# Row transposes moved from TensorE to DMA crossbar transposes, with the down weights loaded in pieces

## The chip, the cores and the metric

The kernel runs on one core of one Trainium2 chip. The metric is the device time of one execution in microseconds (us), as the median of several. All runs compared here are fast runs: a full granted clock (0.98 or more in every run, 1.0 in nearly all).

## The reference

Input `x` has 2048 rows of 640. It is normalised by row, and the result goes two ways: through a two-dimensional Fourier transform, a multiplication by a complex weight for each frequency, and the inverse transform (A); and through two matmuls 640 to 1536 whose results are multiplied, and one back (B).

```python
def _A_ref(x, w_r, w_i):
    X = rfft2(x.astype(float32))            # over rows and columns
    X = X * (w_r + 1j * w_i)
    return irfft2(X, s=(S, D)).astype(bfloat16)

def _B_ref(x, w_gate, w_up, w_down):
    g = einsum("bsd,df->bsf", x, w_gate)    # 2048x640 by 640x1536
    u = einsum("bsd,df->bsf", x, w_up)
    return einsum("bsf,fd->bsd", g * u, w_down)

xn = layernorm(x)
return x + _A_ref(xn, A_w_r, A_w_i) + _B_ref(xn, B_w_gate, B_w_up, B_w_down)
```

## The kernel before

The 2048 rows are 16 row blocks of 128 ("rows 4" below means row block 4). A planner in the kernel takes a list of tasks with estimated durations and priorities and lays them out on the engines when the kernel is built, so a small edit can move many instructions. Everything in SBUF is one allocation, which the profile calls `arena`; PSUM is `ps`. The stages that matter here:

1. Layer norm of each row block on VectorE and ScalarE. Each normalised block is also transposed, since the gate and up matmuls contract over the 640 columns: five transposes by TensorE into PSUM, then one copy into SBUF.

```python
def em_t0(c, b=b):                                   # L813
    for j in range(5):
        ins = c.e.transpose(psb[:, bk * 1024 + j * 128: bk * 1024 + (j + 1) * 128],
                            v_x[:, b, j * 128:(j + 1) * 128], v_sm[:, 0, :])
...
def em_e0(c, b=b, t0=t0):                            # copy helper, L704 on ScalarE
    return copy_on(c, v_xt[:, :, b * 128:(b + 1) * 128], src)
```

2. Gate and up matmuls (L923), 1080 of them, wherever TensorE has nothing more urgent; ScalarE copies the results out and VectorE multiplies them (L938). The first transform runs beside them: VectorE combines rows (L837 to L871) and TensorE multiplies by tables (L884).
3. A loop over 16 frequency tiles: D (L964), weights (VectorE), C (L985 to L988), inverse (L1040, L1041). The inverse needs tables that lie where the down weights will lie later.
4. The down matmuls, two groups of 12 for each row block (L1140). A closing matmul (L1148) adds the inverse transform's result into the same PSUM group. VectorE prepares that result, two row blocks at a time: a matmul I (L1067) into PSUM, a copy, and then the steps V1 to V5 (L1089 to L1122). At last VectorE adds `x` and writes the result out of PSUM (L1155).

```python
b_wd = alloc("WD", 12 * 640)
b_ti = alloc("TI", 16 * 256, at=lay["WD"][0])        # inverse tables share the place
...
dma("ld_wd", v_wd, wdv, 1536 * 1280, [(b_wd, None)], prio=18.0)
...
for ft in range(12):                                 # down group, L1140
    ins = c.e.matmul(ps[:, bk, 0:320], v_ht[:, ft, a * 128:(a + 1) * 128], v_wd[:, ft, sl3],
                     start=(ft == 0), stop=False)
...
return c.e.tensor_tensor(v_out[:, a % 2, sl3], ps[:, bk, 0:320], v_xr[:, xs, sl3], _OP.add)   # L1155
```

Of the kernel before, what the change touches and what calls it, by code (L numbers as in the profile page):

```python
# [498 lines left out]
_X_LOADS = ((0, 1), (1, 1), (2, 1), (3, 1), (4, 4), (8, 8))  # L499
_LN_GROUPS = ((0, 1), (1, 1), (2, 1), (3, 1), (4, 2), (6, 2), (8, 2), (10, 2), (12, 2), (14, 2))  # L500
_NGW = 12
_NW = 4
_GW_LOADS = ((0, 2), (2, 2), (4, 2), (6, 2), (8, 4))
_CHUNKS = ((0, 1), (1, 1), (2, 2), (4, 2), (6, 2), (8, 2), (10, 2), (12, 2), (14, 2))
# [40 lines left out]
def _build(nc, A_x, A_w_r, A_w_i, B_w_gate, B_w_up, B_w_down, out, opts=None):  # L545
# [3 lines left out]
    with es:  # L549
# [19 lines left out]
            return sch.buf(name, off, size)  # L569

        b_ht = alloc("HT", 12 * 2048)
        b_xt = alloc("XT", 5 * 2048)
        b_gw = alloc("GW", 2 * 5 * _NGW * 128)
        b_u = alloc("U", 5 * 2048)
        b_v = alloc("V", 16 * 640, at=lay["U"][0])
        b_z2 = alloc("Z2", 5 * 2048)
        b_x = alloc("X", 16 * 640, at=lay["Z2"][0])
        b_wd = alloc("WD", 12 * 640)
        b_ti = alloc("TI", 16 * 256, at=lay["WD"][0])
        b_g = alloc("G", 640)  # L580
        b_sm = alloc("SM", 384)
        b_gbf = alloc("GBF", 6 * 512)
# [134 lines left out]
        for fi in range(opts.get("nfill", 70)):  # L717
            def em_fill(c):
# [3 lines left out]
                                  stop=True)  # L722
            T("fill%d" % fi, "pe", 2 * _d_mm(128), em_fill, prio=90.0 + 0.001 * fi, bank="single", cls="fill",
              selffree=True, reads=[(b_dum, None)])
        nwarm = opts.get("nwarm", 14)

        def em_warm(c):
            bk = bank_of(c.t)
# [2 lines left out]
                ins = c.e.matmul(ps[:, bk + (i % 2), (i % 4) * 128:(i % 4 + 1) * 128], v_dum[:, 0:128],  # L731
                                 v_dum[:, 128:256], start=True, stop=True)
            return ins
        T("warm", "pe", opts.get("warm_ns", 5200.0), em_warm, reads=[(b_dum, None)], prio=-1.0,
          bank="pair", cls="warm", selffree=True)

        def em_wpad(c):
# [8 lines left out]
        for gi, (b0, nb) in enumerate(_LN_GROUPS):  # L746
# [34 lines left out]

            def em_ve(c, sl_=sl_):
                return c.e.tensor_scalar(v_ve[:, sl_], v_mv[:, sl_, 1], 1e-5, None, _OP.add)
            T("ve_%d" % gi, "dve", 80.0, em_ve, reads=[(b_mv, gk)], writes=[(b_ve, gk)], prio=pbase)

            def em_sd(c, sl_=sl_):
                return c.e.activation(v_sd[:, sl_], v_ve[:, sl_], _ACTF.Sqrt)
            T("sd_%d" % gi, "act", 120.0, em_sd, reads=[(b_ve, gk)], writes=[(b_sd, gk)], prio=pbase)

            def em_rs(c, sl_=sl_):  # L790
                return c.e.reciprocal(v_rs[:, sl_], v_sd[:, sl_])
# [2 lines left out]
            for b in range(b0, b0 + nb):  # L794
                pb = pbase + 0.01 * (b - b0)

                def em_sub(c, b=b):
                    return c.e.tensor_scalar(v_x[:, b, :], v_x[:, b, :], v_mv[:, b, 0:1], None, _OP.subtract)  # L798
                T("sub%d" % b, "dve", 290.0, em_sub, reads=[(b_mv, ("b", b, b + 1))],
                  writes=[(b_x, ("s", b, b + 1))], prio=pb - 0.005)  # L800

                def em_mul(c, b=b):
                    if c.e is nc.scalar:
                        return c.e.activation(v_x[:, b, :], v_x[:, b, :], _ACTF.Copy, scale=v_rs[:, b:b + 1])
                    return c.e.tensor_scalar(v_x[:, b, :], v_x[:, b, :], v_rs[:, b:b + 1], None, _OP.mult)
                muls[b] = T("mul%d" % b, ("dve", "act") if b >= 4 else "dve", {"dve": 290.0, "act": _d_act(640) + 93}, em_mul, reads=[(b_rs, ("b", b, b + 1))],
                  writes=[(b_x, ("s", b, b + 1))], prio=pb)

                def em_t0(c, b=b):
                    bk = bank_of(c.t)  # L810
                    ins = None
                    for j in range(5):
                        ins = c.e.transpose(psb[:, bk * 1024 + j * 128: bk * 1024 + (j + 1) * 128],  # L813
                                            v_x[:, b, j * 128:(j + 1) * 128], v_sm[:, 0, :])
                    return ins
                t0 = T("T0_%d" % b, "pe", 5 * _d_mm(128), em_t0, reads=[(b_x, ("s", b, b + 1)), (b_sm, None)],
                       prio=pb, bank="single", cls="a")

                def em_e0(c, b=b, t0=t0):
                    bk = bank_of(t0)  # L820
                    src = psb[:, bk * 1024: bk * 1024 + 640].rearrange("p (j s) -> p j s", j=5)
                    return copy_on(c, v_xt[:, :, b * 128:(b + 1) * 128], src)
                e0 = T("eT0_%d" % b, ("act", "dve"), {"dve": _d_dve_psum16(640), "act": _d_act(640)}, em_e0,
                       writes=[(b_xt, ("s", b * 128, (b + 1) * 128))], prio=pb - 0.001, frees=t0)
                hold(t0, e0)


# [80 lines left out]
        for ui, (at_, ci, ft0) in enumerate(units):  # L908
            b0, nb = _CHUNKS[ci]
            n = 128 * nb  # L910
            rows = slice(b0 * 128, b0 * 128 + n)
            rr = ui % 3
            pu = 40.0 + 0.005 * ui
            pe_ = 5.0 + 0.001 * ui
            for u in range(2):
                ft = ft0 + u

                def em_gu(c, ft=ft, n=n, rows=rows):
                    bk = bank_of(c.t)
                    ins = None  # L920
                    for w in range(2):
                        for j in range(5):
                            ins = c.e.matmul(ps[:, bk, w * n:(w + 1) * n], v_gw[:, w, j, ft, :],  # L923
                                             v_xt[:, j, rows], start=(j == 0), stop=(j == 4))
                    return ins
                gu = T("GU_%d_%d" % (ft, b0), "pe", 10 * _d_mm(n), em_gu,
                       reads=[(b_gw, ("s", w_ * _NGW + ft, w_ * _NGW + ft + 1)) for w_ in range(2)] + [
                           (b_xt, ("s", b0 * 128, b0 * 128 + n))],
                       prio=pu + 0.001 * u, bank="single", cls="glu")

                def em_eg(c, gu=gu, rr=rr, n=n, u=u):
                    return copy_on(c, v_gbf[:, rr, u, 0:2 * n], ps[:, bank_of(gu), 0:2 * n])
                eg = T("eG_%d_%d" % (ui, u), ("act", "dve"), {"dve": _d_dve_psum(2 * n), "act": _d_act(2 * n)}, em_eg,
                       writes=[(b_gbf, ("r", 2 * rr + u, 2 * rr + u + 1))], prio=pe_, frees=gu)
                hold(gu, eg)

            def em_h(c, ft0=ft0, rr=rr, n=n, rows=rows):
                return c.e.tensor_tensor(v_ht[:, ft0:ft0 + 2, rows], v_gbf[:, rr, :, 0:n], v_gbf[:, rr, :, n:2 * n],  # L938
                                         _OP.mult)
            T("H_%d" % ui, "dve", _d_dve_tt16(2 * n), em_h,  # L940
              reads=[(b_gbf, ("r", 2 * rr, 2 * rr + 2))],
              writes=[(b_ht, ("col", b0, b0 + nb))], prio=pe_)


        dma("ld_ti", v_ti, d_ti, 128 * 16 * 512, [(b_ti, None)], prio=9.0)

        for t in range(16):
            pq = 10.0 + 0.05 * t
# [82 lines left out]
            def em_ia(c, t=t, r2=r2):  # L1031
                bk = bank_of(c.t)
                ins = None
                for k in range(5):
# [5 lines left out]
                    c.e.matmul(dst, l1, v_ti[:, t, 0, :], start=True, stop=False)  # L1040
                    ins = c.e.matmul(dst, l2, v_ti[:, t, 1, :], start=False, stop=True)  # L1041
                return ins
            ia = T("IA_%d" % t, "pe", 10 * _d_mm(128), em_ia, reads=[(b_y, ("r", 2 * r2, 2 * r2 + 2)), (b_ti, None)],
                   prio=pq, bank="pair", cls="a")

            def em_eia(c, ia=ia, t=t):
# [5 lines left out]
            hold(ia, eia)  # L1052


        dma("ld_wd", v_wd, wdv, 1536 * 1280, [(b_wd, None)], prio=18.0)
        for a in range(16):
            pa = 19.0 + 0.05 * a
            pc = 41.0 + 0.05 * a
# [68 lines left out]
        for a in range(16):  # L1127
# [4 lines left out]
            for hf in range(2):  # L1132
# [3 lines left out]
                def em_ag2(c, a=a, sl3=sl3):  # L1136
                    bk = bank_of(c.t)
                    ins = None
                    for ft in range(12):
                        ins = c.e.matmul(ps[:, bk, 0:320], v_ht[:, ft, a * 128:(a + 1) * 128], v_wd[:, ft, sl3],  # L1140
                                         start=(ft == 0), stop=False)
                    return ins
                ag2 = T("ACC_%d_%d" % (a, hf), "pe", 12 * _d_mm(320), em_ag2,
                        reads=[(b_ht, ("col", a, a + 1)), (b_wd, None)],
# [100 lines left out]
```

## Time and profile before

| | before |
|---|---|
| timed | 214.1 us median of 3 (214.05 to 214.6) |
| span of the profiled run | 212.6 us |
| TensorE | 2116 matmuls, busy 207.1 us (97%) |
| VectorE, ScalarE | busy 185.8 us (87%), 128.5 us (60%) |
| last first-transform matmuls start | 83.57 us |
| last inverse matmul done | 139.92 us |
| first down matmul | 149.23 us |

The prediction shows the lines of the engine table, the chain of waits and TensorE's timeline.

### The profile page before, as it was taken

To read this page: it belongs to the slowest core of one execution; us is meant where nothing else is said; L and a number is where in the kernel's file an instruction comes from. 1 tells how busy PE (TensorE), PEld (TensorE's weight loads), DVE (VectorE), ACT (ScalarE), POOL (GpSimd) and SP (SyncE) were. 2 spreads that over 40 slices of the span, in tenths; PEclk is the share of its full clock that TensorE was granted. 3 is DMA by queue.
4 is the path that set the end of the run, shared out by engine and by line. 5 is a ranking of instruction groups with operands and counts; after the bars stand their busy time and mean duration, and the time that the engine had idled before them with its cause. 6 is when DMAs were issued, how large, how long until landed. Compare 5 with 4: busy or idle time off the path is not lost.

```text
span 212.6 us, 5325 instructions
## 1 busy us (share of the span) xinstructions
PE 207.1 (97%) x2116; PEld 174.9 (82%) x2116; DVE 185.8 (87%) x535; ACT 128.5 (60%) x292; POOL 0.2 (0%) x4
## 2 busy tenths in 40 slices
PE   8999999999999999999999999999999999999994
PEld 8999899987878989889898888999767767777773
DVE  3599999999999997499999999839999999999621
ACT  2476899999998776779899888787212220200000
POOL 0000000000000000000000000000000000000000
DMA  6999991000000000012222220039112322333211
GB/s 191 303 341 392 393 294 33 0 0 3 0 5 0 3 0 0 3 38 59 56 58 53 57 55 9 3 100 375 39 46 80 108 79 63 108 96 101 84 48 46
DMA packets 22184, 19.78 MB, mean 93 GB/s; under 512 B 2192, under 2 KB 21264, under 8 KB 21904
## 3 DMA queue, kind: packets, MB, share of 16 engines
q1 hardware_dynamic: 20048, 18.37, 29.2%
q10 hardware_dynamic: 2112, 1.08, 1.9%
q8 instruction: 16, 0.26, 0.5%
q14 instruction: 8, 0.07, 0.1%
HBM read 16.82 MB, written 2.62 MB: 91 GB/s over the span
## 4 chain that ended last, share of the span: by engine, by line
PE 79%; DVE 17%; ACT 1%; issue 1%; DVEq 0%
PE ps L923 38%; PE ps L1140 21%; PE ps L731 3%; PE ps L1041 2%; PE ps L1040 2%; PE ps L1067 2%; PE ps L964 2%; DVE arena L938 2%; PE ps L1148 2%; PE ps L884 1%; DVE arena L837 1%; PE ps L813 1%; DVE arena L798 1%; PE ps L985 1%; PE ps L988 1%; PE ps L987 1%
## 5 line engine op out<-in xcount | busy, mean ns | idle before, releaser
L704 ACT ACTIVATE arena<-ps 128x512 bf16<-128x512 f32 (+5 forms) x200 | 107.1, 584 | 50.0 <-PE ps L1067 26.1
L923 PE MATMUL ps<-arena 128*128 128x256 bf16 (+1 forms) x1080 | 113.5, 261 | 0.8 <-ACT arena L704 0.8
L923 PEld LDWEIGHTS ps<-arena 128*128 128x128 bf16 x1080 | 93.6, 98 | 11.3 <-ACT arena L704 1.9
L1140 PE MATMUL ps<-arena 128*128 128x320 bf16 x384 | 56.7, 299 | 0.0
L1140 PEld LDWEIGHTS ps<-arena 128*128 128x128 bf16 x384 | 37.3, 98 | 14.2
L938 DVE TENSOR_TENSOR arena<-arena 128x512 bf16<-128x512 bf16 (+1 forms) x54 | 20.9, 390 | 10.0 <-ACT arena L704 9.7
L1000 DVE TENSOR_TENSOR arena<-ps,arena 128x256 f32<-128x256 f32 x64 | 22.6, 418 | 0.0
L1155 DVE TENSOR_TENSOR arena<-ps,arena 128x320 bf16<-128x320 f32 x32 | 15.5, 485 | 8.1 <-PE ps L1148 8.1
L1041 PE MATMUL ps<-arena 128*128 128x128 bf16 x80 | 10.6, 219 | 0.0
L1040 PE MATMUL ps<-arena 128*128 128x128 bf16 x80 | 10.6, 219 | 0.0
L1148 PE MATMUL ps<-arena 128*128 128x320 bf16 x32 | 9.6, 299 | 0.0
L1040 PEld LDWEIGHTS ps<-arena 128*128 128x128 bf16 x80 | 8.8, 112 | 0.4
L837 DVE TENSOR_TENSOR arena<-arena 128x384 f32<-128x384 bf16 x16 | 8.9, 554 | 0.0
L1041 PEld LDWEIGHTS ps<-arena 128*128 128x128 bf16 x80 | 8.7, 113 | 0.1
L731 PE MATMUL ps<-arena 128*128 128x128 bf16 x56 | 6.1, 313 | 1.0 <-DVE arena L738 1.0
L1003 DVE TENSOR_TENSOR arena<-ps,arena 128x260 f32<-128x260 f32 x16 | 7.1, 444 | 0.0
L1015 DVE TENSOR_TENSOR arena<-arena 128x256 bf16<-128x256 f32 x16 | 6.8, 423 | 0.2
L1024 ACT ACTIVATE arena<-arena 128x256 bf16<-128x256 bf16 x16 | 6.6, 415 | 0.3 <-DVE arena L1019 0.2
L757 ACT ACTIVATE arena<-arena 128x640 bf16<-128x640 bf16 x8 | 6.8, 845 | 0.0
L731 PEld LDWEIGHTS ps<-arena 128*128 128x128 bf16 x56 | 5.9, 150 | 1.0 <-DVE arena L738 1.0
L838 DVE TENSOR_TENSOR arena<-arena 128x256 f32<-128x256 bf16 x16 | 6.7, 421 | 0.0
L1019 DVE TENSOR_TENSOR arena<-arena 128x256 bf16<-128x256 f32 x16 | 6.7, 420 | 0.0
(71 smaller groups left out, 224.2 us busy)
## 6 DMA issues: line engine op xcount, KB each, us to landing
arena<-in_A_x_dram SPq DMA_DIRECT2D x20, 160.0 KB, 3.0
out_dram<-arena SPq DMA_DIRECT2D x32, 80.0 KB, 1.6
arena<-in_B_w_down_dram SPq DMA_DIRECT2D x1, 1920.0 KB, 9.1
arena<-c_tf SPq DMA_DIRECT2D x4, 384.0 KB, 11.2
arena<-in_A_w_r_dram SPq DMA_DIRECT2D x32, 40.1 KB, 2.2
arena<-in_A_w_i_dram SPq DMA_DIRECT2D x32, 40.1 KB, 2.2
arena<-in_B_w_gate_dram SPq DMA_DIRECT2D x4, 320.0 KB, 7.5
arena<-in_A_x_dram SPq DMA_DIRECT2D x1, 1280.0 KB, 12.1
```

The lines of the kernel that those rows point to most:

```text
L704: return c.e.activation(dst, src, _ACTF.Copy)
L731: ins = c.e.matmul(ps[:, bk + (i % 2), (i % 4) * 128:(i % 4 + 1) * 128], v_dum[:, 0:128], v_dum[:, 128:256], start=True, stop=True)
L837: c.e.tensor_tensor(uo[:, o, :, 0:3, :], v_xb[:, b:b + 2, 0:6:2, :], v_xb[:, b:b + 2, 5:10:2, :], op)
L923: ins = c.e.matmul(ps[:, bk, w * n:(w + 1) * n], v_gw[:, w, j, ft, :], v_xt[:, j, rows], start=(j == 0), stop=(j == 4))
L938: return c.e.tensor_tensor(v_ht[:, ft0:ft0 + 2, rows], v_gbf[:, rr, :, 0:n], v_gbf[:, rr, :, n:2 * n], _OP.mult)
L1000: c.e.tensor_tensor(v_p[:, r2, w, :, 128 * h:128 * h + 128].rearrange("p c (m k) -> p c m k", k=4), xh.rearrange("p c (m k) -> p c m k", k ...
L1003: ins = c.e.tensor_tensor(v_p[:, r2, :, :, 256:321], ps[:, bk:bk + 2, 256:321].unsqueeze(1).to_broadcast([128, 2, 2, 65]), v_w[:, wr, :, 0 ...
L1040: c.e.matmul(dst, l1, v_ti[:, t, 0, :], start=True, stop=False)
L1041: ins = c.e.matmul(dst, l2, v_ti[:, t, 1, :], start=False, stop=True)
L1140: ins = c.e.matmul(ps[:, bk, 0:320], v_ht[:, ft, a * 128:(a + 1) * 128], v_wd[:, ft, sl3], start=(ft == 0), stop=False)
L1148: return c.e.matmul(ps[:, bank_of(ag2), 0:320], v_sm[:, 2, :], v_v[:, a, sl3], start=False, stop=True)
L1155: return c.e.tensor_tensor(v_out[:, a % 2, sl3], ps[:, bk, 0:320], v_xr[:, xs, sl3], _OP.add)
```

## The change

Its intent: take 60 of the 80 row transposes and their copies off TensorE, ScalarE and VectorE, and let the DMA crossbar do them from SBUF to SBUF. With less TensorE work in front, fewer gate and up matmuls are left to cover the late load of the down weights, so that load is cut: 800 KB (tiles 7 to 11) go early into the part that the inverse tables leave free, the rest follows in four pieces as the tables are used up. Third, the transposes of rows 0 and 1 are copied out by ScalarE (two tiles) and VectorE (three) at once, into separate buffers, and the warm-up is 8 matmuls shorter.

```diff
+_WD_LOADS = ((7, 12), (0, 2), (2, 4), (4, 6), (6, 7))
+_FT_ORDER = (7, 8, 9, 10, 11, 0, 1, 2, 3, 4, 5, 6)
...
-        nwarm = opts.get("nwarm", 14)
+        nwarm = opts.get("nwarm", 12)
...
+                if b >= opts.get("xt_dma", 4):
+                    def em_xt(c, b=b):
+                        return c.e.dma_start_transpose(v_xt[:, :, b * 128:(b + 1) * 128], v_x[:, b, :])
+                    T("xt%d" % b, "sp", opts.get("xt_issue", 1500.0), em_xt, reads=[(b_x, ("s", b, b + 1))],
+                      writes=[...], prio=pb, nbytes=128 * 1280)
+                    continue
...
+                if b < opts.get("e0_split", 2):
+                    for part, (j0, j1) in (("act", (0, 2)), ("dve", (2, 5))):
+                        def em_e0s(c, b=b, t0=t0, j0=j0, j1=j1):
...
+                            return copy_on(c, v_xt[:, j0:j1, b * 128:(b + 1) * 128], src)
...
-        dma("ld_wd", v_wd, wdv, 1536 * 1280, [(b_wd, None)], prio=18.0)
+        for f0, f1 in _WD_LOADS:
+            dma("ld_wd%d" % f0, v_wd[:, f0:f1], wdv[:, f0:f1], 128 * (f1 - f0) * 1280,
+                [(b_wd, ("e", 640 * f0, 640 * f1))], prio=18.0 if f0 < 7 else 9.6)
...
-                    for ft in range(12):
+                    for ft in _FT_ORDER:
```

Left out: the load of the inverse tables in two halves, finer dependencies on the tables, and slightly earlier priorities for two tiny layer-norm steps. In the changed kernel the same code has other line numbers: row transposes L828, crossbar transposes L816, gate and up L951, first transform L912, inverse L1070 and L1071, I L1099, V1 to V5 L1121 to L1154, down L1172, closing L1180, result L1187.

More of the change, by code (lines that the diff above doesn't have):

```diff
@@ L571, in _build @@
         b_ht = alloc("HT", 12 * 2048)
-        b_xt = alloc("XT", 5 * 2048)
+        b_xta = alloc("XTA", 2 * 2048)
+        b_xtb = alloc("XTB", 3 * 2048)
+        lay["XT"] = (lay["XTA"][0], 5 * 2048)
         b_gw = alloc("GW", 2 * 5 * _NGW * 128)
@@ L578, in _build @@
         b_wd = alloc("WD", 12 * 640)
-        b_ti = alloc("TI", 16 * 256, at=lay["WD"][0])
+        b_ti = b_wd
+        lay["TI"] = (lay["WD"][0], 16 * 256)
         b_g = alloc("G", 640)
@@ L733, in em_warm @@
             return ins
-        T("warm", "pe", opts.get("warm_ns", 5200.0), em_warm, reads=[(b_dum, None)], prio=-1.0,
+        T("warm", "pe", opts.get("warm_ns", 5050.0), em_warm, reads=[(b_dum, None)], prio=-1.0,
           bank="pair", cls="warm", selffree=True)
@@ L783, in em_ve @@
                 return c.e.tensor_scalar(v_ve[:, sl_], v_mv[:, sl_, 1], 1e-5, None, _OP.add)
-            T("ve_%d" % gi, "dve", 80.0, em_ve, reads=[(b_mv, gk)], writes=[(b_ve, gk)], prio=pbase)
+            T("ve_%d" % gi, "dve", 80.0, em_ve, reads=[(b_mv, gk)], writes=[(b_ve, gk)], prio=pbase - 0.006)
             def em_sd(c, sl_=sl_):
                 return c.e.activation(v_sd[:, sl_], v_ve[:, sl_], _ACTF.Sqrt)
-            T("sd_%d" % gi, "act", 120.0, em_sd, reads=[(b_ve, gk)], writes=[(b_sd, gk)], prio=pbase)
+            T("sd_%d" % gi, "act", 120.0, em_sd, reads=[(b_ve, gk)], writes=[(b_sd, gk)], prio=pbase - 0.006)
             def em_rs(c, sl_=sl_):
@@ L807, in _build @@
                   writes=[(b_x, ("s", b, b + 1))], prio=pb)
+                if b >= opts.get("xt_dma", 4):
+                    def em_xt(c, b=b):
+                        return c.e.dma_start_transpose(v_xt[:, :, b * 128:(b + 1) * 128], v_x[:, b, :])
+                    T("xt%d" % b, "sp", opts.get("xt_issue", 1500.0), em_xt, reads=[(b_x, ("s", b, b + 1))],
+                      writes=[(b_xta, ("s", b * 128, (b + 1) * 128)), (b_xtb, ("s", b * 128, (b + 1) * 128))], prio=pb, nbytes=128 * 1280)
+                    continue
                 def em_t0(c, b=b):
@@ L812, in em_t0 @@
                     for j in range(5):
-                        ins = c.e.transpose(psb[:, bk * 1024 + j * 128: bk * 1024 + (j + 1) * 128],
+                        o_ = j * 128
+                        if b < opts.get("e0_split", 2):
+                            o_ = j * 128 if j < 2 else 1024 + (j - 2) * 128
+                        ins = c.e.transpose(psb[:, bk * 1024 + o_: bk * 1024 + o_ + 128],
                                             v_x[:, b, j * 128:(j + 1) * 128], v_sm[:, 0, :])
@@ L816, in _build @@
                 t0 = T("T0_%d" % b, "pe", 5 * _d_mm(128), em_t0, reads=[(b_x, ("s", b, b + 1)), (b_sm, None)],
-                       prio=pb, bank="single", cls="a")
+                       prio=pb, bank="pair" if b < opts.get("e0_split", 2) else "single", cls="a")
+                if b < opts.get("e0_split", 2):
+                    for part, (j0, j1) in (("act", (0, 2)), ("dve", (2, 5))):
+                        def em_e0s(c, b=b, t0=t0, j0=j0, j1=j1):
+                            bk = bank_of(t0)
+                            o_ = bk * 1024 + (1024 if j0 else 0)
+                            src = psb[:, o_: o_ + (j1 - j0) * 128].rearrange("p (j s) -> p j s", s=128)
+                            return copy_on(c, v_xt[:, j0:j1, b * 128:(b + 1) * 128], src)
+                        n_ = (j1 - j0) * 128
+                        es_ = T("eT0_%d_%s" % (b, part), part, {"dve": _d_dve_psum16(n_), "act": _d_act(n_)}, em_e0s,
+                                writes=[(b_xta if j0 == 0 else b_xtb, ("s", b * 128, (b + 1) * 128))], prio=pb - 0.001, frees=t0)
+                    hold(t0, es_)
+                    continue
                 def em_e0(c, b=b, t0=t0):
@@ L823, in _build @@
                 e0 = T("eT0_%d" % b, ("act", "dve"), {"dve": _d_dve_psum16(640), "act": _d_act(640)}, em_e0,
-                       writes=[(b_xt, ("s", b * 128, (b + 1) * 128))], prio=pb - 0.001, frees=t0)
+                       writes=[(b_xta, ("s", b * 128, (b + 1) * 128)), (b_xtb, ("s", b * 128, (b + 1) * 128))], prio=pb - 0.001, frees=t0)
                 hold(t0, e0)
@@ L927, in _build @@
                        reads=[(b_gw, ("s", w_ * _NGW + ft, w_ * _NGW + ft + 1)) for w_ in range(2)] + [
-                           (b_xt, ("s", b0 * 128, b0 * 128 + n))],
+                           (b_xta, ("s", b0 * 128, b0 * 128 + n)), (b_xtb, ("s", b0 * 128, b0 * 128 + n))],
                        prio=pu + 0.001 * u, bank="single", cls="glu")
@@ L942, in _build @@
               writes=[(b_ht, ("col", b0, b0 + nb))], prio=pe_)
-        dma("ld_ti", v_ti, d_ti, 128 * 16 * 512, [(b_ti, None)], prio=9.0)
+        for q in range(2):
+            dma("ld_ti%d" % q, v_ti[:, 8 * q:8 * q + 8], d_ti[:, 8 * q:8 * q + 8], 128 * 8 * 512,
+                [(b_wd, ("e", 2048 * q, 2048 * q + 2048))], prio=9.0 + 0.3 * q)
         for t in range(16):
@@ L1042, in em_ia @@
                 return ins
-            ia = T("IA_%d" % t, "pe", 10 * _d_mm(128), em_ia, reads=[(b_y, ("r", 2 * r2, 2 * r2 + 2)), (b_ti, None)],
+            ia = T("IA_%d" % t, "pe", 10 * _d_mm(128), em_ia, reads=[(b_y, ("r", 2 * r2, 2 * r2 + 2)), (b_wd, ("e", 256 * t, 256 * t + 256))],
                    prio=pq, bank="pair", cls="a")
@@ L1138, in em_ag2 @@
                     ins = None
-                    for ft in range(12):
+                    for ft in _FT_ORDER:
                         ins = c.e.matmul(ps[:, bk, 0:320], v_ht[:, ft, a * 128:(a + 1) * 128], v_wd[:, ft, sl3],
-                                         start=(ft == 0), stop=False)
+                                         start=(ft == 7), stop=False)
                     return ins
```

## The prediction

> **What bounds the kernel now.** I read the page's table of engines first, then its chain, then the waits of TensorE, then the timeline of TensorE with its gaps added up by hand.
>
> ```profile
> span 212.6 us, 5325 instructions
> ...
> PE 207.1 (97%) x2116; PEld 174.9 (82%) x2116; DVE 185.8 (87%) x535; ACT 128.5 (60%) x292; POOL 0.2 (0%) x4
> ...
> PE 79%; DVE 17%; ACT 1%; issue 1%; DVEq 0%
> ```
>
> TensorE is nearly always busy and carries 79% of the chain. Busy time of pipelined matmuls is not work, though, so I count start to start, from the timeline:
>
> ```profile
> 22.83 3.44 PE L923 MATMUL ps<-arena 128*128 128x256 bf16 x30
> 26.11 0.72 PE L813 MATMUL ps<-arena 128*128 128x128 bf16 x10
> 26.66 6.44 PE L923 MATMUL ps<-arena 128*128 128x256 bf16 x90
> 32.94 0.72 PE L884 MATMUL ps<-arena 128*128 128x128 bf16 x10
> ```
>
> Columns are start, length, engine, line, shape, count. Thirty gate/up matmuls 256 wide take 26.11 - 22.83 = 3.28 us, 109 ns each; ten 128 wide (row transposes, L813) 26.66 - 26.11 = 0.55, 56 ns each; in the same way 136 ns for 320 or 321 columns. With the counts of the program: gate/up 840 x 0.109 + 240 x 0.056 = 105.1; down 416 x 0.136 = 56.6; row transposes 80 x 0.056 = 4.5; the other transforms 400 x 0.056 + 64 x 0.1365 = 31.1; fillers 20 x 0.056 = 1.1. Sum 198.3 us. The warm-up (56 matmuls, start 1.05 to the first row transpose at 7.18) takes 6.1. The last matmul ends at 209.98, so 209.98 - 1.05 - 198.3 - 6.1, some 4.5 us, is all that TensorE loses over the whole run, and the rest after it is a 2.6 us tail. No large wait is left to remove: only work, and small stalls. Named waits are tiny:
>
> ```profile
> PE ps L731 <- DVE arena L738: 1.0, 1, 1.0
> PE ps L923 <- ACT arena L704: 0.8, 2, 0.6
> PE ps L1067 <- DVE arena L1099: 0.5, 1, 0.5
> ```
>
> Second bound: VectorE. From 33 to 62 us it is as full as TensorE, and ScalarE too:
>
> ```profile
> core 0: us, PE busy (x) PEld busy (x) DVE busy (x) ACT busy (x) POOL busy (x), PEclk, DMA share, GB/s
> ...
> 33.00:62.00 29.00, 28.73 (x297) 24.69 (x295) 28.76 (x94) 28.52 (x65) 0.00 (x0) 1.00 0.01 3
> 62.00:86.00 24.00, 24.00 (x246) 21.48 (x244) 21.33 (x56) 18.30 (x33) 0.00 (x0) 1.00 0.00 1
> ```
>
> VectorE's chain of layer norm and first transform (L837 to L871) ends about 83.0 us, and the last first-transform matmuls (L884) follow at 83.57: VectorE paces the start of the loop over frequency tiles, and TensorE stays full only because gate/up matmuls fill in.
>
> **What the Trainium skill says.** "VectorE: DVE Perf Modes", The three transpose paths, gives 1309 ns for a 128x128 bf16 transpose by the DMA crossbar and 390 ns by TensorE. In this trace TensorE's transposes are pipelined at 56 ns, so the measurement decides there; no run so far shows a crossbar transpose. "Advanced Engine Details and Errata", X-Bar Transpose (TRN2), says that transposes run as fast as ordinary DMAs, 350 to 400 GB/s. The two pages differ by more than ten for one row block of five tiles (6.5 us against 0.5 us), which is my largest uncertainty. "DMA: Bandwidth & Descriptors", Issuing engines are not separate DMA queues, says that all DMAs share the same 16 engines; the trace agrees in that the inverse tables, issued at 17.6 us, land 15.2 us later, behind everything before them. "TensorE: Matmul & The Clock Gate", Part 1, says the array runs at half rate until about 3.4 us of sustained work; here the warm-up runs at 109 ns per 128-wide matmul (half rate) up to about 6.9 us, so it takes longer than the page says.
>
> **The change, part by part.**
>
> Transposes removed: 12 rows x 5 = 60 matmuls x 56 ns = 3.36 us of TensorE, on the path. Their copies out of PSUM, some 12 x 0.6 us, were nearly all ScalarE's; that relieves an engine that is full from 33 to 62 us and may give back some 0.3 us of hidden stalls, no more. VectorE gains nothing: the built order of instructions gives it 3 copies of first transposes (two of three tiles, about 0.27 us each, one of five, 0.40) where it had two (0.80).
>
> Start: 8 warm-up matmuls fewer x 109 ns = 0.87 us. The first normalised row is ready at 5.98 us (L805 at 5.59, 0.39 long), so the first transpose can start at 6.3, though at half rate (0.55 us in place of 0.28). Its copy is split: ScalarE took 0.70 us (7.50 to 8.20). VectorE's part stands behind row 1's statistics, which end about 7.2 us, so it ends near 7.5, and gate/up starts near 7.6 instead of 8.41. Row 1's normalisation then waits 0.27 us for that copy, so part is given back in the layer-norm chain. I count 0.6 us.
>
> Down weights: before, one load of 1920 KB is issued at 140.1 us, after the last use of the inverse tables, and lands 9.1 us later. TensorE covers that with 70 gate/up matmuls, 7.6 us, so it costs nothing now. In the changed order only 30 gate/up matmuls stand after the last inverse matmul; the other 40 go before the frequency loop. So the piecewise load is what makes the removal usable rather than a gain itself. The last piece (160 KB; loads of that size land in 3.0 us) depends on the last inverse matmul; TensorE has 10 + 10 + 10 gate/up and 20 inverse matmuls (3.3 + 1.1 = 4.4 us) before the first down matmul: hidden.
>
> Loop over frequency tiles: 300 gate/up matmuls lie in it in both orders, with the same VectorE work: unchanged.
>
> Where the loop starts: TensorE work before the last first-transform matmuls is 510 x 0.109 instead of 470 x 0.109 (+4.4 us), minus 3.36, minus 0.6: it arrives where it did before, about 83.7. VectorE's work up to there, summed from the built order with the trace's durations, is 0.8 us more (two more gate/up products of 0.34 and the copy), 0.3 us earlier at best: about 83.5 to 84. So the loop starts within 0.5 us of where it did, near 84.1 at the end of those matmuls. From there the old kernel took 209.98 - 84.12 = 125.86 us; 40 gate/up matmuls fewer, 4.4 us: 121.5. End 205.6, plus the 2.6 tail: span 208.2. The timed median exceeded the profiled span by 1.5 us (214.1 - 212.6): **209.7 us**. The other way round: 4.5 - (3.36 + 0.6 = 4.0) leaves the same small losses as before.
>
> **The rivals.**
>
> A: the first crossbar transposes come late. They stand on the queue behind all loads, now with 800 KB of down weights among them. DMA traffic before drains at 32.5 us:
>
> ```profile
> 31.50:32.00 0.50, 0.50 (x13) 0.50 (x10) 0.48 (x2) 0.38 (x3) 0.00 (x0) 1.00 1.14 171
> 32.00:32.50 0.50, 0.50 (x12) 0.41 (x9) 0.50 (x3) 0.33 (x2) 0.00 (x0) 1.00 0.62 116
> 32.50:33.00 0.50, 0.50 (x12) 0.50 (x11) 0.40 (x2) 0.50 (x2) 0.00 (x0) 1.00 0.35 86
> ```
>
> The second last column is the DMA share, the last GB/s. 0.82 MB at 390 GB/s adds 2.1 us: about 34.7. Rows 4 and 5 then land near 37 if a transpose moves as a copy does. Gate/up of these rows starts after 29.6 us of TensorE work from the first transpose; with the first-transform matmuls of rows 2 and 3 held by VectorE to about 33.5, that is 36.8 to 37.4. So a stall of 0 to 1.5 us, in full on the path: 209.7 to 211.2. For it: the transposes are issued after their loads. Against: the later ones have 10 us and more to spare.
>
> B: crossbar transposes at 1.3 us per tile, one after another: row 4 lands about 41, row 5 near 48, a stall of some 11 us: about 221. The later rows need one pair per 14 us and would just keep up. I give it 1 in 20.
>
> C: VectorE becomes the bound: TensorE's saving returns as waits before the frequency loop and in the last transform (L1089 to L1122), where TensorE lost 0.7 us between 150 and 160 with more filler than it has now. If half the saving goes there: 211.7. Against: TensorE now has three down groups ahead of the first closing matmul, so 9.9 us after the last inverse matmul, and VectorE needed 10.0 with two more products in between.
>
> D: everything goes well, the stalls in 47 to 61 and at 160 us go too: 208.3.
>
> **Range and chances.** 209.7, with A and C to the upper side more than D to the lower: 208.2 to 213.0. Faster by 2% means under 209.8, right at my number: 0.46 faster, 0.49 the same, 0.05 slower (B).
>
> **What would show it right or wrong.** The row transposes should fall to 20, 60 matmuls fewer. TensorE's first gate/up near 7.6 us. At the first gate/up of rows 4 and 5 (about 37 us) there should be at most a wait of 1.5 us on a crossbar transpose; time from issue to landing of these should be 2 to 5 us. The last first-transform matmuls near 84 us. The first down matmul some 4.4 us after the last inverse one, without a wait on a load. A wait over 3 us on a crossbar transpose, or idle TensorE before L1187's partner matmuls (L1180), would make the number wrong.

## The result, and the profile after

The changed kernel takes 213.21 us (median of 4, 212.72 to 213.35), the kernel before in the same rounds 214.18 us (median of 4). The ratio is 0.9947, with a 95% interval of 0.9925 to 0.9969. Ratios and intervals here are worked out from all fast runs of the same rounds, so a ratio is not quite that of the medians quoted. The change wins about 1 us where 4.4 were predicted. It is "the same" at the 2% bar, and the time lies 0.2 us above the range of 208.2 to 213.0 that was given.

The page of the changed kernel, engine table and chain by engine:

```profile
span 211.5 us, 5204 instructions
...
PE 202.6 (96%) x2044; PEld 169.4 (80%) x2044; DVE 185.1 (87%) x536; ACT 122.1 (58%) x281; POOL 0.2 (0%) x4
...
PE 67%; DVE 22%; DMA 6%; issue 3%; ACT 1%; SPq 0%; DVEq 0%
```

TensorE has 72 matmuls fewer (60 transposes, 8 of warm-up, 4 fillers), so the work did go. But the chain carries 67% of TensorE in place of 79%, 22% of VectorE in place of 17%, and 6% of DMA, which was not in it before. Removed work came back as waits, and those have names. TensorE's waits (total, times, longest) in the changed kernel:

```profile
PE ps L951 <- DMA arena<-arena: 1.2, 1, 1.2
...
PE ps L951 <- DVE arena L775: 0.9, 1, 0.9
PE ps L1099 <- DVE arena L1131: 0.7, 2, 0.4
...
PE ps L1180 <- DVE arena L1154: 0.4, 1, 0.4
PE ps L1172 <- DVE arena L1187: 0.3, 1, 0.3
```

**The start.** TensorE and VectorE in the first ten microseconds, two answers of the timeline:

```profile
5.88 0.44 PE L828 MATMUL ps<-arena 128*128 128x128 bf16 x5 [0.55 <-DVE arena L810]
...
8.16 1.28 PE L951 MATMUL ps<-arena 128*128 128x128 bf16 x20 [0.95 <-DVE arena L775]
```

```profile
6.87 0.49 DVE L769 BATCH_NORM_STATS2 arena<-arena 128x6 f32<-128x320 bf16 x1 [1.14 <-DMA arena<-in_A_x_dram]
7.28 0.48 DVE L770 BATCH_NORM_STATS2 arena<-arena 128x6 f32<-128x320 bf16 x1
7.68 0.34 DVE L710 COPY arena<-ps 128x384 bf16<-128x384 bf16 x1
```

The first row's transposes start at 5.88 us, 1.1 us earlier than before (6.99). Gate and up start at 8.16 where before had 8.41: only 0.25 us is left. TensorE's wait is put down to L775, the short step that follows on VectorE, but what was missing is the copy L710 at 7.68. It stands behind row 1's two statistics in VectorE's order, and these waited 1.14 us for row 1's load. VectorE was free all that time, and the tiles that it had to copy were in PSUM from about 6.3 (5.88 + 0.44).

This is one execution of each kernel, and the start differs from one to the next. In the five other profiles with the same split (e1, e3, e4, e5 and e6 below), row 1's load lands earlier and gate and up start at 7.65 to 7.83; in e8, which has the start of the kernel before, they start at 7.64 and not at 8.41. By the first pair of first-transform matmuls, with the same gate/up matmuls and row transposes in front of it in both kernels, the difference is 0.32 us:

```profile
22.27 0.72 PE L884 MATMUL ps<-arena 128*128 128x128 bf16 x10
21.95 0.72 PE L912 MATMUL ps<-arena 128*128 128x128 bf16 x10
```

**The crossbar.** TensorE where rows 4 and 5 are due and at the last first-transform matmuls (these in the kernel before as well, L884), and the crossbar transposes by themselves (issue time on the queue in ns as minimum, median and maximum, then first and last start; below it issue to landing):

```profile
34.43 3.44 PE L951 MATMUL ps<-arena 128*128 128x256 bf16 x30
39.07 6.91 PE L951 MATMUL ps<-arena 128*128 128x256 bf16 x60 [1.21 <-DMA arena<-arena]
45.91 0.73 PE L912 MATMUL ps<-arena 128*128 128x128 bf16 x10
...
85.37 0.72 PE L912 MATMUL ps<-arena 128*128 128x128 bf16 x10
```

```profile
83.57 0.72 PE L884 MATMUL ps<-arena 128*128 128x128 bf16 x10
```

```profile
L816 SPq DMA_TRANSPOSE arena<-arena x12: 1200/1210/1721, 32.2 to 66.5; - x12
DMA to landing us min/median/max: 2.6/2.7/6.5
```

TensorE stands still for 1.21 us. The last first-transform matmuls, at 83.57 before, start at 85.37, so the loop starts 1.8 us later. The landing of 6.5 us is that of the first transpose (the second takes 5.1); the median is 2.7. The wait, too, differs between executions: e4 and e6, with the same order in this part, show 0.7 us of it and last first-transform matmuls at 84.71 and 84.89.

**The loop.** From the end of those matmuls to the last inverse matmul, before took 139.92 - 84.12 = 55.80 us and the changed kernel takes 141.71 - 85.93 = 55.78.

**The end.** The last inverse matmul to the start of the last closing matmul: 209.57 - 139.92 = 69.65 us before, 208.54 - 141.71 = 66.83 after. TensorE's work there, start to start: 415 down and closing matmuls x 0.1358 = 56.36, 80 of I x 0.056 = 4.48, and gate/up 70 x 0.109 = 7.63 before, 30 x 0.109 = 3.27 after. So the work is 68.5 and 64.1 us, and TensorE loses 1.2 us before and 2.7 after. The 1.2 us before are three gaps, all in front of the matmuls I (L1067, at 152.95, 159.51 and 173.28). Busy time of each engine (length of the stretch, PE, PEld, DVE, ACT, POOL, clock, DMA share, GB/s), first before:

```profile
150.00:170.00 20.00, 19.45 (x160) 14.07 (x159) 19.83 (x48) 3.93 (x7) 0.00 (x0) 1.00 0.23 67
170.00:190.00 20.00, 19.88 (x159) 14.45 (x157) 19.97 (x50) 2.60 (x4) 0.00 (x0) 1.00 0.30 87
```

and after:

```profile
150.00:170.00 20.00, 18.74 (x153) 13.17 (x152) 19.93 (x50) 3.90 (x6) 0.00 (x0) 1.00 0.25 74
170.00:190.00 20.00, 19.54 (x155) 14.00 (x154) 19.96 (x49) 2.60 (x4) 0.00 (x0) 1.00 0.27 79
```

VectorE is full in both kernels. What differs is whether TensorE has other work meanwhile. In the changed kernel the chain runs on VectorE from 153.8 to 189.2 us, and TensorE waits in small pieces, like this first one at the second pair of row blocks:

```profile
158.11 0.45 PE L1180 MATMUL ps<-arena 128*128 128x320 bf16 x2 [0.41 <-DVE arena L1154]
```

Before, TensorE reached its first down matmul at 149.23 and VectorE's first pair was ready at 149.88 (L1122 ends), only 0.65 us behind. After, TensorE comes at 146.10 and VectorE's first pair is ready at 151.04 (L1154 ends), 4.9 us behind:

```profile
149.23 1.80 PE L1140 MATMUL ps<-arena 128*128 128x320 bf16 x12
149.46 0.42 DVE L1122 TENSOR_TENSOR arena<-arena 128x256 bf16<-128x256 f32 x1
146.10 1.79 PE L1172 MATMUL ps<-arena 128*128 128x320 bf16 x12
150.62 0.42 DVE L1154 TENSOR_TENSOR arena<-arena 128x256 bf16<-128x256 f32 x1
```

The first two lines are of the kernel before, the others of the changed one. VectorE needs 6.74 us for a pair (L1123 at 158.65, then 165.39) and TensorE 52 x 0.1358 + 10 x 0.056 = 7.62, so VectorE makes up some 0.9 us in each pair, and the waits end only after several pairs.

So the theory was: 1.8 us are lost before the loop (crossbar wait and start) and 1.5 us at the end (VectorE's pace). The rivals: the crossbar itself is too slow, or the removed transposes cost nothing before, since VectorE paces everything.

### The profile page after: what moved, and what is told of

It is laid out like the page before. It is cut to its first block, busy times and chain, and to the rows that moved or that the text cites. A ratio compares the mean times of both kernels' runs of the same rounds, so it can differ in the third digit from the quotient of the medians.

```text
span 211.5 us, 5204 instructions
## 1 busy us (share of the span) xinstructions
PE 202.6 (96%) x2044; PEld 169.4 (80%) x2044; DVE 185.1 (87%) x536; ACT 122.1 (58%) x281; POOL 0.2 (0%) x4
## 4 chain that ended last, share of the span: by engine, by line
PE 67%; DVE 22%; DMA 6%; issue 3%; ACT 1%; SPq 0%; DVEq 0%
PE ps L951 41%; PE ps L1172 12%; DMA arena<-arena 3%; DMA arena<-in_A_x_dram 2%; PE ps L1070 2%; PE ps L1071 2%; DVE arena L1187 2%; PE ps L994 2%; PE ps L912 2%; DVE arena L1144 1%; DVE arena L1145 1%; DVE arena L1153 1%; DVE arena L1137 1%; PE ps L1015 1%; ACT arena L709 1%
## 5 line engine op out<-in xcount | busy, mean ns | idle before, releaser
L709 ACT ACTIVATE arena<-ps 128x512 bf16<-128x512 f32 (+5 forms) x189 | 99.9, 572 | 55.0 <-PE ps L1099 28.2
L951 PE MATMUL ps<-arena 128*128 128x256 bf16 (+1 forms) x1080 | 112.8, 261 | 2.8 <-DMA arena<-arena 1.2
L951 PEld LDWEIGHTS ps<-arena 128*128 128x128 bf16 x1080 | 93.6, 98 | 14.2 <-ACT arena L709 1.6
L1172 PE MATMUL ps<-arena 128*128 128x320 bf16 x384 | 56.5, 299 | 0.3 <-DVE arena L1187 0.3
L1172 PEld LDWEIGHTS ps<-arena 128*128 128x128 bf16 x384 | 37.2, 98 | 14.7 <-DVE arena L1187 0.7
L1187 DVE TENSOR_TENSOR arena<-ps,arena 128x320 bf16<-128x320 f32 x32 | 15.4, 482 | 6.7 <-PE ps L1180 6.7
L1071 PE MATMUL ps<-arena 128*128 128x128 bf16 x80 | 10.7, 219 | 0.0
L1070 PE MATMUL ps<-arena 128*128 128x128 bf16 x80 | 10.6, 219 | 0.0
L1180 PE MATMUL ps<-arena 128*128 128x320 bf16 x32 | 9.1, 300 | 0.5 <-DVE arena L1154 0.4
L1070 PEld LDWEIGHTS ps<-arena 128*128 128x128 bf16 x80 | 8.7, 112 | 0.5
L1071 PEld LDWEIGHTS ps<-arena 128*128 128x128 bf16 x80 | 8.7, 112 | 0.1
L769 DVE BATCH_NORM_STATS2 arena<-arena 128x6 f32<-128x320 bf16 x8 | 3.9, 489 | 3.8 <-DMA arena<-in_A_x_dram 3.7
L1152 DVE TENSOR_TENSOR arena<-arena 128x640 bf16<-128x640 f32 x8 | 6.5, 818 | 0.1
(71 smaller groups left out, 212.2 us busy)
## 6 DMA issues: line engine op xcount, KB each, us to landing
arena<-c_ti SPq DMA_DIRECT2D x2, 512.0 KB, 14.5
```

The source lines that it names most:

```text
L709: return c.e.activation(dst, src, _ACTF.Copy)
L951: ins = c.e.matmul(ps[:, bk, w * n:(w + 1) * n], v_gw[:, w, j, ft, :], v_xt[:, j, rows], start=(j == 0), stop=(j == 4))
L1070: c.e.matmul(dst, l1, v_ti[:, t, 0, :], start=True, stop=False)
L1071: ins = c.e.matmul(dst, l2, v_ti[:, t, 1, :], start=False, stop=True)
L1180: return c.e.matmul(ps[:, bank_of(ag2), 0:320], v_sm[:, 2, :], v_v[:, a, sl3], start=False, stop=True)
```

## The experiments

Eight kernels were run, in two sets of four. In the first the kernel before had a median of 214.32 us (11 runs), in the second 214.45 us (11 runs). All the edits but the last are to the changed kernel, which was not run again in these sets: a gain over it is a comparison across sets, by the ratios to the kernel before (its own is 0.9947, 0.9925 to 0.9969). Where the intervals overlap, as for e2 and e3, the times alone do not show a difference from it.

| run | median us (runs) | ratio to before | 95% interval |
|---|---|---|---|
| e1_late_down | 212.35 (6) | 0.9905 | 0.9885 to 0.9925 |
| e2_whole_copy | 212.56 (6) | 0.9917 | 0.9893 to 0.9940 |
| e3_no_xbar | 213.89 (6) | 0.9973 | 0.9953 to 0.9993 |
| e4_short_tail | 210.62 (5) | 0.9817 | 0.9793 to 0.9841 |
| e5_one_down | 214.52 (4) | 1.0032 | 0.9997 to 1.0068 |
| e6_act_out | 212.12 (5) | 0.9896 | 0.9879 to 0.9913 |
| e7_all_three | 211.05 (4) | 0.9841 | 0.9826 to 0.9856 |
| e8_before_act_out | 215.41 (6) | 1.0056 | 1.0037 to 1.0076 |

### e1_late_down: the early down piece behind the crossbar transposes

```diff
-                [(b_wd, ("e", 640 * f0, 640 * f1))], prio=18.0 if f0 < 7 else 9.6)
+                [(b_wd, ("e", 640 * f0, 640 * f1))], prio=18.0 if f0 < 7 else 9.6, after=[muls[15]] if f0 == 7 else [])
```

The 800 KB load is issued after the last normalisation, so after the 12 transposes. The built order of TensorE, VectorE and ScalarE is unchanged; one row of the queue moved.

> The changed kernel with one difference: the early piece of the down weights (800 KB) is issued after the twelve crossbar transposes instead of before them; the order on TensorE, VectorE and ScalarE is instruction for instruction that of the changed kernel. Theory A (the transposes stand behind that load, and TensorE's wait for them is on the path to the end): the first transpose lands about 4.4 us after its issue instead of 6.5, TensorE's wait of 1.2 us before the gate/up matmuls of rows 4 and 5 goes, and the time falls from 213.2 to about 212.0. Rival (VectorE's chain paces that stretch anyway): the wait goes, but the fourth pair of first-transform matmuls still starts near 53.6 us and the time stays within 0.3 us of 213.2.

Measured: 212.35 us. The line of the changed kernel with its 1.21 us wait becomes one unbroken run of 90 matmuls:

```profile
34.34 10.39 PE L951 MATMUL ps<-arena 128*128 128x256 bf16 x90
...
84.28 0.72 PE L912 MATMUL ps<-arena 128*128 128x128 bf16 x10
```

The first transposes are issued at 30.33 us in place of 32.16, and no wait on a crossbar transpose is left in the list. The loop starts 1.09 us earlier (84.28 for 85.37), and the end after it takes 66.84 us, as before the edit. This profile also starts gate and up earlier (7.75 for 8.16), but by 34 us that has shrunk to 0.09 us, so about 1.0 us is the crossbar's. So the wait came from the place of one load on a queue, and it was passed on to the end nearly in full. The detail was missed: the first two transposes still take 5.8 and 4.6 us from issue to landing, not the 4.4 expected, so most of the gain is the earlier issue. e5 below, where that load is not there at all before the loop, agrees: no crossbar wait, and last first-transform matmuls at 84.33.

### e2_whole_copy: no split of the first copies

```diff
-                        if b < opts.get("e0_split", 2):
+                        if b < opts.get("e0_split", 0):
```

(the same at the two other places of the option). ScalarE copies the first two rows' transposes alone. The shorter warm-up stays. The planner also moves some later work: the first-transform matmuls of rows 2 and 3 come 20 gate and up matmuls later.

> The changed kernel with the first two transposed rows copied out whole, as before the change, and the short warm-up kept. Theory (VectorE's part of the split copy stands behind row 1's statistics, so the split holds TensorE up rather than freeing it): gate/up starts near 7.1 us instead of 8.16. Whether that survives: VectorE also loses 2 x 0.27 us of copies, so I expect the first-transform matmuls of rows 0 and 1 0.3 to 0.5 us earlier and a time of about 212.8. Rival (rows 1 to 3 are paced by their loads and layer norm): the early start is waited away by the third row transpose and the time stays at 213.2.

Measured: 212.56 us. TensorE's first gate and up:

```profile
7.35 1.28 PE L951 MATMUL ps<-arena 128*128 128x128 bf16 x20
```

They start 0.81 us earlier than with the split (8.16), and without a wait in the line. The last first-transform matmuls start at 84.64, 0.73 us earlier, and the end takes the same time (66.85). The crossbar wait is still 1.3 us.

The 0.73 us are not all the split's. At the first pair of first-transform matmuls only 0.29 us of the 0.81 are left:

```profile
21.66 0.73 PE L912 MATMUL ps<-arena 128*128 128x128 bf16 x10
```

It is 21.95 in the changed kernel and 21.79 to 21.99 in the five other profiles with the split; e7 below, without it, has 21.98. The rest comes between 44 and 54 us, where TensorE's pauses, from start to start, add up to 0.9 us in the changed kernel and to 0.3 here: that is where the planner's other order of the first-transform matmuls lies. So the split wins nothing: it keeps three of row 0's five tiles waiting in VectorE's order behind statistics that wait for a load. But what it costs is at most some 0.3 us, and the larger part of this run's gain goes with the planner's moves. By the times alone, the intervals of this run and of the changed kernel overlap.

### e3_no_xbar: all transposes on TensorE, the rest of the change kept

```diff
-                if b >= opts.get("xt_dma", 4):
+                if b >= opts.get("xt_dma", 16):
```

> The changed kernel with rows 4 to 15 transposed on TensorE again; warm-up, split copies and piecewise down weights as changed. 60 matmuls (3.36 us) come back to TensorE, and the planned order has again 70 gate/up matmuls after the last inverse matmul. Theory (most of what the crossbar saves is lost again in waits: 1.2 us for the first transposes, 1.5 us in the last transform where TensorE waits for VectorE): those two waits go, and the time is about 213.8, 0.5 us above the changed kernel. Rival (the crossbar gives its 3.4 us and something else in the change costs): 216.

Measured: 213.89 us, as expected. TensorE has 2104 matmuls, the planner again leaves 70 gate and up matmuls after the last inverse matmul, and from there to the last closing matmul it takes 209.03 - 139.38 = 69.65 us, as before. The start and the pieces alone win 0.4 us of 214.32, and the profile agrees: the last first-transform matmuls start at 83.04, 0.53 us before those of the kernel before. By the ratios (0.9947 of the changed kernel, in another set, against 0.9973) the crossbar transposes win some 0.6 us, of 3.36 us of TensorE work that they remove; the two intervals overlap, so this gain is not clear of the noise.

### e4_short_tail: less VectorE work in the last transform

```diff
-                c.e.tensor_tensor(v_vb[:, b_:b_ + 2, 0:10:2, :], e0, e1, _OP.add)
+                if opts.get("v5_full", 0):
+                    c.e.tensor_tensor(v_vb[:, b_:b_ + 2, 0:10:2, :], e0, e1, _OP.add)
```

One addition of 0.75 us for each pair of row blocks is left out; the result is wrong.

> The changed kernel, wrong result on purpose: one VectorE addition per row pair of the last transform (0.75 us, 8 of them) is left out; all orders are otherwise those of the changed kernel. Theory C (after 150 us TensorE waits for VectorE, 1.5 to 1.8 us in all): these waits go and the time falls to about 211.6. Rival (TensorE is held there by its own order or by PSUM banks, not by VectorE's work): the time stays above 212.7.

Measured: 210.62 us, more than expected. From the last inverse matmul to the last closing one it takes 205.27 - 141.05 = 64.22 us, 2.6 less than the changed kernel, where TensorE's work is 64.1. So TensorE loses 0.1 us there, and no wait on VectorE after 150 us is left in the list. All but 0.1 us of what TensorE loses in this stretch is thus VectorE's pace. (The crossbar wait in its profiled run was 0.7 us, so a little of the rest is chance.)

### e5_one_down: the down weights in one load

```diff
-_WD_LOADS = ((7, 12), (0, 2), (2, 4), (4, 6), (6, 7))
+_WD_LOADS = ((0, 12),)
```

> The changed kernel with the down weights in one load after the last inverse matmul, as before the change; crossbar transposes, short warm-up and split copies as changed. Theory (the pieces are what makes the crossbar usable: only 30 gate/up matmuls are left to cover the load): that load lands about 9.1 us after the last inverse matmul, TensorE has 3.3 + 1.7 = 5.0 us of work to cover it, so it waits about 4 us for it; VectorE's last transform runs on meanwhile, so the 1.5 to 2 us of waits for VectorE after 150 us mostly go. Net +2 to +2.5 us on the changed kernel: about 215.5. Rival (the load is covered by the last transform's matmuls): 213.2.

Measured: 214.52 us, 1.3 over the changed kernel by the medians, though its four runs scatter (213.96 to 216.21). The two longer ones had a slightly lower granted clock (0.992 and 0.984); the two at the full clock, 213.96 and 213.97, are 0.75 us over it, and the profiled spans differ by 0.7 (212.2 and 211.5). The cost of 2 to 2.5 us that was expected did not come.

```profile
PE ps L1172 <- DMA arena<-in_B_w_down_dram: 2.3, 1, 2.3
```

```profile
149.09 1.80 PE L1172 MATMUL ps<-arena 128*128 128x320 bf16 x12 [2.27 <-DMA arena<-in_B_w_down_dram]
```

From the last inverse matmul to the first down matmul it takes 149.09 - 140.69 = 8.4 us with 5.0 us of work, so TensorE stands still for 3.4 us (4 expected; the load landed in 8.2 us and not 9.1). Two things make the cost smaller than that. VectorE works on meanwhile, so the later waits on it are shorter: to the last closing matmul it takes 209.12 - 140.69 = 68.43 us, 1.6 more than the changed kernel's 66.83. And the expectation overlooked that this edit also takes the early piece away from in front of the crossbar transposes: no crossbar wait is left, and the loop starts 1.04 us earlier (84.33 for 85.37). So the pieces are worth 1.6 us at the end, and their early part cost 1.0 us where it stood on the queue. Against the kernel before the ratio is 1.0032, with 1 inside the interval: without the pieces no gain of the crossbar transposes is to be seen.

### e6_act_out: ScalarE takes the results out of PSUM

```diff
-                    return c.e.tensor_tensor(v_out[:, a % 2, sl3], ps[:, bk, 0:320], v_xr[:, xs, sl3], _OP.add)
+                def em_f0(c, ag2=ag2, a=a, sl3=sl3):
+                    return c.e.activation(v_out[:, a % 2, sl3], ps[:, bank_of(ag2), 0:320], _ACTF.Copy)
...
+                    return c.e.tensor_tensor(v_out[:, a % 2, sl3], v_out[:, a % 2, sl3], v_xr[:, xs, sl3], _OP.add)
```

ScalarE, nearly idle at the end, copies each result to SBUF; VectorE adds `x` there in bf16. The Trainium skill, "VectorE: DVE Perf Modes", section Rules for kernel authors, says that elementwise work on a matmul's output runs at the single rate from PSUM, while bf16 in SBUF reaches a double rate for tensor_tensor. This case agrees in direction: the addition takes 0.40 us from start to start from PSUM and 0.23 to 0.24 from SBUF.

> The changed kernel with the results taken out of PSUM by ScalarE, idle in that stretch (32 copies of 320 columns), and the input added by VectorE from SBUF in bf16; a right result, one more rounding. VectorE does about 0.24 instead of 0.40 us for each (5 us less in all), and PSUM banks no longer wait for VectorE's place in its order. Theory C (VectorE sets the pace from 150 to 189 us): TensorE's waits there fall below 0.7 us and the time to about 211.2; the end is 0.2 us longer behind the last matmul. Rival (the run without one addition was faster only because the last transform's chain itself was shorter, which this leaves as long): no better than 212.7.

Measured: 212.12 us. A pair takes VectorE 6.26 us in place of 6.74. From the last inverse matmul to the last closing one it takes 206.84 - 141.24 = 65.60 us, 1.2 less, so TensorE loses 1.5 us there in place of 2.7. The size was missed by half, and the profile says why. TensorE's loss was to fall below 0.7 us, but the planner now puts the matmuls I every three down groups, which is 3 x 13 x 0.1358 + 10 x 0.056 = 5.9 us of TensorE work, less than VectorE's 6.26, so TensorE waits 0.2 to 0.4 us at each:

```profile
159.38 0.73 PE L1099 MATMUL ps<-arena 128*128 128x128 bf16 x10
165.63 0.73 PE L1099 MATMUL ps<-arena 128*128 128x128 bf16 x10 [0.17 <-DVE arena L1131]
```

And after the start of the last closing matmul there are 210.3 - 206.84 = 3.5 us in place of 211.5 - 208.54 = 3.0, since the last result now passes two engines.

### e7_all_three: e1, e2 and e6 together

> The changed kernel with the three mends together: early piece of the down weights after the crossbar transposes, first transposes copied out whole by ScalarE, results taken out by ScalarE. If the three causes are separate and each on the path, the gains add: 213.2 - 0.9 - 0.7 - 2.0 = about 209.6, which is what the prediction had. If VectorE's chain before the frequency loop swallows the first two together, 210.5 to 211.

Measured: 211.05 us, ratio 0.9841, and the result is correct: 3.4 us under the kernel before and 2.2 under the changed one. By medians the single gains over the changed kernel are 0.86, 0.65 and 1.09, 2.6 in sum, so they nearly add; the 209.6 that was expected did not come. The last first-transform matmuls start at 83.74 and end at 84.30 us; the planner's order of e2 is part of that. What is left at the start has another cause, row 1's normalisation, which comes late:

```profile
PE ps L828 <- DVE arena L810: 1.6, 2, 0.8
```

### e8_before_act_out: the same evacuation in the kernel before

The edit of e6, made in the kernel before. It asks whether VectorE's pace at the end was a cost there too.

> The kernel before with only its results taken out of PSUM by ScalarE and the input added from SBUF. Theory C says that VectorE's pace in the last transform costs that kernel only the 0.5 to 0.7 us of waits its trace shows, less 0.2 us of longer end: about 213.9 where the kernel before has 214.3. If it gains 2 us here as well, then the waits are not something that the change made.

Measured: 215.41 us, ratio 1.0056: slower, where a small gain was expected. The end takes 210.16 - 139.75 = 70.41 us (69.65 before). In the kernel before, TensorE had 70 gate and up matmuls to do while VectorE got ahead, and lost only 1.2 us there; here it loses 1.9, because the planner puts the matmuls I every three down groups, as in e6, and also waits 0.2 us for the down weights. So the run does not separate VectorE's work from the planner's order. What it shows is that no 2 us were to be had here. That the change raised the loss at the end rests on the two profiles (1.2 and 2.7 us) and on e3, which leaves the end at 69.65 us as in the kernel before.

## Why the prediction was wrong

The mechanism was named: rivals A and C were in the prediction, and both came true at once, while the central number assumed that neither would. Step by step:

- **Transposes removed, 3.36 us: right.** 60 fewer, and the 20 left run at 56 ns each.
- **"I count 0.6 us" for the start: about right, but not for the reason given.** In the pair of profiles 0.32 us of it is there at the first first-transform matmuls (21.95 for 22.27); e3, with the new start and no crossbar, starts the loop 0.53 us earlier than the kernel before. "Gate/up starts near 7.6" came true in five of six profiles (7.65 to 7.83); in that of the changed kernel it was 8.16, since row 1's load landed late. The split adds nothing (e2). And the 109 ns for each warm-up matmul that is left out belong to one execution: there the warm-up ran at half rate to its end, while in e8, which has the same start, the full rate came 2.9 us sooner. The guess that the first transposes would run "at half rate (0.55 us in place of 0.28)" failed here for the same reason: five took 6.16 - 5.88 = 0.28.
- **"So the loop starts within 0.5 us of where it did, near 84.1": this step failed.** The last first-transform matmuls ended at 85.93. Of the 1.8 us, 1.0 to 1.1 is rival A's crossbar wait (e1 takes it away and gains 1.09 there; e5 gains 1.04). Another 0.4 us is a slip in the sum: 83.57 + 4.4 - 3.36 - 0.6 is 84.0 for their start, not "about 83.7". It shows in the total too, since a gain of 214.1 - 209.7 = 4.4 us was forecast from 3.36 + 0.6 = 3.96 us of work taken away. The last 0.3 us is the part of the 0.6 for the start that this profile does not show. With e1, e2 and e6 together it is 84.30 (e7), near where the prediction had put it, but with the help of the planner's other order. The rival's mechanism was right (first transposes issued behind loads, wait of 0 to 1.5 us, measured 1.2); it should have stood in the central number, since the argument for it was a position on a queue that the built order shows.
- **"Loop over frequency tiles: unchanged": right,** to 0.02 us.
- **"40 gate/up matmuls fewer, 4.4 us: 121.5": this step failed too.** Between the start of the loop and the last matmul it took 123.0 (208.54 + 0.41 - 85.93, with the same 0.41 from start to end as before). The matmuls did go, but 1.5 us of waits on VectorE came: rival C. The prediction counted 9.9 us after the last inverse matmul for TensorE against 10.0 for VectorE and called it even. That is true of the first closing matmul (151.54, no wait in its line) and says nothing of the second pair: what counts is the lead that VectorE has. In the kernel before it was 0.65 us behind TensorE's first down matmul; in the changed one it is 4.9 us behind. e4 shows that the loss is all VectorE's pace, and e6 nearly halves it. It was there before as well, but smaller: 1.2 us against 2.7.
- **Down weights "hidden": right,** first down matmul 146.10 - 141.71 = 4.4 us after the last inverse one, without a wait on a load. And they are needed: e5.
- **Rival B: refuted.** A row block of five tiles lands in 2.7 us at the median, no later row waits. **Rival D** did not come.

The sum: 209.7 + 1.8 + 1.5 = 213.0, measured 213.21. Nothing of size is left to explain in this pair of profiles; single executions differ by half a microsecond at the start and at the crossbar wait. Two small readings of the prediction were off as well: the first row transpose starts at 6.99 in the timeline (the 7.18 is the chain's), and the warm-up's matmuls come every 107 ns. Left open: whether the planner's order alone would give the larger part of e2's gain, which no run separates, and why the first two crossbar transposes take 5 to 6.5 us where later ones take 2.7; other loads are in flight at that time, but no run separated it.

## What to carry to other kernels

When work is taken off a full engine, ask at each point where it meets another engine how far ahead that one is: a partner with 87% busy and no lead turns saved work into waits. On a queue with loads of different urgency the order of issue is part of the critical path; one load moved behind the urgent ones was worth nearly as much as the whole change. A copy split over two engines ends with the slower one, so look at what stands in front of each half before splitting. And an early gain seen in two profiles is not a gain at the end: follow it to the next point where the engines meet, and look at how much that point moves between executions of one kernel.

## What the Trainium skill lacked or had wrong

- "VectorE: DVE Perf Modes", The three transpose paths: its 1309 ns for one 128x128 tile by the crossbar must not be multiplied by the tiles. Here five tiles (one 128x640 bf16 block, SBUF to SBUF, one instruction) land 2.7 us after issue at the median (the first two of the changed kernel took 6.5 and 5.1), and TensorE's transposes follow each other every 56 ns where the page has 390 for one.
- "Advanced Engine Details and Errata", X-Bar Transpose (TRN2): "as fast as regular DMAs" fits better (in the changed kernel loads of 160 KB of `x` land in 2.6 us at the median, transposes of 160 KB in 2.7), but this is the time to landing of small transfers; no run here measured a bandwidth.
- No page gives this chip's measured issue time on the queue for a crossbar transpose of such a block (the table in "DMA: Bandwidth & Descriptors" that counts cycles for it is about trn3, with figures of "previous generations" beside it, for other sizes): here 1200 ns at least and 1210 at the median, so the twelve need 14.5 us of the queue.
- "TensorE: Matmul & The Clock Gate", Part 1: the page puts the step to the full rate at around 4 us of sustained work, 500 ns more or less from run to run. Here it varies more: the warm-up's matmuls go from one every 107 ns to one every 56 ns after 3.1 us in the profile of the changed kernel and after 6.0 us in that of the kernel before, and the other eight profiles lie between 2.7 (e5) and 5.3 us (e4). The profile's clock column reads 1.00 at both rates. So a gain counted from the length of a warm-up in one execution holds for that execution.
